# One conditional weight cast less in the slot loop of an attention and two-layer expert kernel

## The chip, the cores and the metric

The kernel runs on one core of a Trainium2 chip. The metric is the device time of one execution in microseconds (us). Engines are named as in the profile: PE (TensorE; PEld are its weight loads), DVE (VectorE), ACT (ScalarE), POOL (GpSimd), SP (SyncE, which here only issues transfers). A q behind a name is that engine's instruction queue: its branches and semaphore instructions.

## What is computed

A gated linear attention over 4 x 8 heads of 768 steps gives 3072 tokens of 384 values. A dense layer with three first matrices follows, and then a layer of eight experts, of which every token uses one:

```python
h = np.maximum(np.maximum(x @ w1, x @ w2), x @ w3)       # dense layer
x = h @ w_out
e_idx = np.argmax(x @ w_gate, axis=1)                      # expert of a token
for e in range(E):
    mask = e_idx == e
    h = np.maximum(x[mask] @ w1[e], 0.0)                   # 384 -> 1024
    out[mask] = gate_w[mask, None] * eom[mask, e, None] * (h @ w2[e])   # 1024 -> 384
```

## The kernel before

The attention and the dense layer take the first 480 us or so and are not touched. Then the tokens are sorted by expert into up to 31 slots of 128 rows; a slot holds tokens of one expert only. The slots are worked off in the order of the program text (a manual schedule: each engine executes its instructions in the order in which the code traces them).

For accuracy a float32 product is made of three products of split parts: every weight w becomes a high part (a cast on ACT, L605) and a low part (a subtraction on DVE, L606). `split1` does that for the 3 x 1024 first-layer weights of an expert in six pieces, from the landing tile s1a or s1b into w1H and w1L; `split2` does it for the second layer in eight pieces, from s2a or s2b into w2H and w2L. There is one pair w1H, w1L and one pair w2H, w2L. They are rewritten only at a slot with a new expert, under an `If`.

The last slot of an expert may hold fewer than 64 tokens. Such a slot is of kind 1 and runs alone: it multiplies the unsplit float32 weights in the landing tiles directly, in two halves of the PE array, and needs no cast. `by_kind` chooses between the two forms with an `If` on PE, ACT and DVE.

The stages of a slot j are:

- `gather` (POOL): fetch its rows; `stage` (SP): fetch its expert's weights, when they are new
- `tx`: three transposes on PE (L788), then high and low part of the rows on ACT (L793) and DVE (L794)
- `up(j, 0)` and `up(j, 1)`: first layer, columns 0 to 511 and 512 to 1023, nine matmuls each (L825), and a copy out of PSUM by ACT (L826). For a slot that runs alone the first does nothing and the second does the whole layer (L814, copy L834)
- `th`: eight transposes on PE (L865; alone L870), then `cut`: Relu on ACT (L844) and the low part on DVE (L845)
- `down`: second layer, 24 matmuls (L884; alone L814), the scaling on ACT (L898) and a scatter by POOL (L904)

They are interleaved over three slots. In iteration j of the loop the text has, in this order: `split2` pieces 0 and 1 of slot j, if new (L1152); `up(j+1, 0)`; `th(j)`; `split2` pieces 2 to 7 (L1162); the early call `cast1(j+2, 2)` (L1165); `up(j+1, 1)`; `tx(j+2)`; the fetch of s1 for slot j+3; the late call `cast1(j+2, 1)` (L1174); `down(j)`; the fetch of s2 for slot j+2.

`cast1(j, when)` is an `If` (L1132) around `split1(j)`, taken where `new[j]` equals `when`. `new[j]` is made in `slots_e` from the routing: 0 for a slot with the old expert or one that runs alone; 2 for a slot with a new expert behind a slot that runs alone; 1 for a new expert behind any other slot. The early place is open only behind a slot that runs alone, because such a slot does not read w1H and w1L. An `If` that is not taken sends, on each of its engines' queues, the semaphore signals that its body would have sent, so that whoever waits for the body goes on.

The whole program stands twice in the text, a second time for inputs with large decays; that second part is not executed here.

Of the kernel before, what the change touches and what calls it, by code (L numbers as in the profile page):

```python
# [18 lines left out]
ALU = mybir.AluOpType  # L19
# [14 lines left out]
NS = NT + NE - 1  # L34
# [50 lines left out]
def layers(tc, pool, wk, K, general, *args):  # L85
    with ExitStack() as ctx:
        _layers(ctx, tc, pool, wk, K, general, *args)


def _layers(ctx, tc, pool_, wk, K, general, qk, al, a0, v, vT, w123, wout, gates, ew1, ew2, out):  # L90

    nc = tc.nc
# [3 lines left out]
    oh, oc, rmod, rdiv, pri, io128, ioS, ioF, ut, ones, one8, pid, tno, meta, kinds, first, e0, gidx, sidx = (  # L96
        K[n] for n in ("oh", "oc", "rmod", "rdiv", "pri", "io128", "ioS", "ioF", "ut", "ones", "one8", "pid", "tno", "meta", "kinds",
                       "first", "e0", "gidx", "sidx"))
# [391 lines left out]
    def wt(shape, name, dt=F32):  # L490
        return wk.tile(shape, dt, tag=name, name=name)
# [86 lines left out]
    xg, cx, cxF, hs, ch, chg, new, eos, kind = ({} for _ in range(9))  # L578
# [29 lines left out]
    def split1(j, pieces=range(6)):  # L608
        for n in pieces:
            split(*(t[:, n % 3, n // 3 * 512:(n // 3 + 1) * 512] for t in (C["s1"][j % 2], *C["w1"])))  # L610

    def split2(j, pieces=range(NE)):
        for f in pieces:
            split(*(t[:, f] for t in (C["s2"][j % 2], *C["w2"])))
# [122 lines left out]
    def slots_e():  # L737

        end = rtmp["end"]
        rem = wt([128, NE], "rem", I32)  # L740
        nc.vector.tensor_single_scalar(rem, rtmp["ci"], 127, op=ALU.bitwise_and)
        few = wt([128, NE], "few")
        nc.vector.tensor_single_scalar(few, rem, 64.0, op=ALU.is_lt)
        lst = wt([128, NE], "lst")
        nc.vector.scalar_tensor_tensor(lst, end, isf, nfirst, op0=ALU.subtract, op1=ALU.mult)
        nc.vector.scalar_tensor_tensor(lst, end, -1.0, lst, op0=ALU.add, op1=ALU.subtract)
        wide = [128, NS, NE]
        le = wt(wide, "le", BF16)
        nc.vector.tensor_tensor(le, lst.unsqueeze(1).to_broadcast(wide), ioS.unsqueeze(2).to_broadcast(wide), ALU.is_equal)
        nc.vector.tensor_tensor(le, le, few.unsqueeze(1).to_broadcast(wide), ALU.mult)  # L750
        kd = wt([128, NS], "ff")
        nc.vector.tensor_reduce(kd, le, op=ALU.add, axis=AX.X)
        nc.vector.tensor_copy(kinds[:, :NS], kd)


        nc.vector.tensor_tensor(kinds[:, 2 * NS:], meta[:, NS:2 * NS], kd, ALU.max)
        when = wt([128, NS + 1], "eo")
        nc.vector.memset(when[:, 0:1], 1.0)
        nc.vector.tensor_scalar_add(when[:, 1:], kd, 1.0)
        nc.vector.scalar_tensor_tensor(when[:, :NS], kd, 0.0, when[:, :NS], op0=ALU.is_equal, op1=ALU.mult)  # L760
        nc.vector.tensor_tensor(kinds[:, NS:2 * NS], when[:, :NS], meta[:, NS:2 * NS], ALU.mult)

    def load_meta(j):
        chg[j] = nc.values_load(kinds[0:1, 2 * NS + j:2 * NS + j + 1], engines=(ET.SP,), min_val=0, max_val=1)
        eos[j] = nc.values_load(meta[0:1, j:j + 1], engines=(ET.SP,), min_val=0, max_val=NE - 1)

    def load_kind(j):
        kind[j] = nc.values_load(kinds[0:1, j:j + 1], engines=(ET.PE, ET.Activation, ET.DVE),
                                 min_val=0, max_val=1)
        new[j] = nc.values_load(kinds[0:1, NS + j:NS + j + 1], engines=(ET.Activation, ET.DVE),  # L770
                                min_val=0, max_val=2)

    def stage(j, both=((0, "s1"), (1, "s2"))):
        for n, s in both:
            nc.sync.dma_start(out=C[s][j % 2], in_=(ew1, ew2)[n][ds(eos[j], 1)].rearrange("o p a b -> p (o a) b"),
                              cond=(chg[j] == 1))

    def gather(j):
        xg[j] = C["cr"].tile([128, XW], F32, tag="xg", name="xg", bufs=4)
        n = TF * 128 if j < NF else NTOK  # L780
        nc.gpsimd.indirect_dma_start(out=xg[j], out_offset=None, in_=x2d[:n, :],
                                     in_offset=bass.IndirectOffsetOnAxis(ap=gidx[:, j:j + 1], axis=0),
                                     bounds_check=n - 1, oob_is_err=False)

    def tx(j):
        ps = bank(C["psT"], "T", "psT")
        for k in range(3):
            nc.tensor.transpose(ps[:, k * 128:(k + 1) * 128], xg[j][:, k * 128:(k + 1) * 128], ident)  # L788
        cx[j] = bp.tile([128, 2, DM], F32R, tag=("xH", "xL")[j % 2], name="cx")
        cxF[j] = bp.tile([128, DM], F32, tag="hH", name="cxF", bufs=7)  # L790

        def parts(hi, lo, p):
            nc.scalar.copy(hi, p)  # L793
            nc.vector.tensor_sub(lo, p, hi.bitcast(F32))  # L794

        def alone():
            nc.scalar.copy(cxF[j], ps[:, :DM])

        by_kind(j, lambda: parts(cx[j][:, 0], cx[j][:, 1], ps[:, :DM]), alone)
# [75 lines left out]
    def down(j, fs=(0, NE)):  # L875
        if fs[0] == 0:
            C["dn"] = bank(psM, "M", "psP") if j == 1 else bank(psO, "O", "psP")
        ps = C["dn"]
        w2H, w2L = C["w2"]

        def whole():
            for f in range(*fs):
                for n, (x, w) in enumerate(((0, w2H), (0, w2L), (1, w2H))):
                    mm(ps[:, :DM], ch[j][:, x, f * 128:(f + 1) * 128], w[:, f], start=(f + n == 0),  # L884
                       stop=(f == NE - 1 and n == 2))

        def alone():
            w = C["s2"][j % 2]
            for f in range(4):
                x = hs[j][:, 512 + f * 128:512 + (f + 1) * 128]  # L890
                halves(ps, DM, (x[:, :64], x[:, 64:]), (w[:, f], w[:, f + 4]), f == 0, f == 3)

        by_kind(j, whole, alone)
        if fs[1] < NE:
            return
        y = bp.tile([128, DM], F32, tag="hm", name="yo")
        gate = xg[j][:, DM:XW]
        nc.scalar.activation(y, ps[:, :DM], AF.Copy, scale=gate)  # L898
        if j in kind:
            with tc.If(kind[j] > 0):  # L900
                t = bp.tile([128, DM], F32, tag="hL", name="ylo", bufs=7)
                nc.scalar.copy(t[:64], ps[64:, :DM])
                nc.vector.scalar_tensor_tensor(y[:64], t[:64], gate[:64], y[:64], op0=ALU.mult, op1=ALU.add)
        nc.gpsimd.indirect_dma_start(out=out[:, :], out_offset=bass.IndirectOffsetOnAxis(ap=sidx[:, j:j + 1], axis=0),  # L904
                                     in_=y, in_offset=None, bounds_check=NTOK - 1, oob_is_err=False)
# [205 lines left out]
    then(slots_d)  # L1111
    then(down, 0)
    then(slots_e)

    with tc.manual_schedule() if not general else nullcontext():
# [12 lines left out]
    def guard(j):  # L1128
        return tc.If(n_all > j) if j >= NT else nullcontext()

    def cast1(j, when):
        with tc.If(new[j] == when):  # L1132
            split1(j)

    down(1, (0, 2))
# [3 lines left out]
    up(2, 0)  # L1139
    up(2, 1)  # L1140
    load_kind(NF + 1)
    load_kind(NF + 2)
    n_all = nc.values_load(meta[0:1, 2 * NS:2 * NS + 1], min_val=0, max_val=NS)
    tx(3)
    cast1(3, 1)
    down(1, (5, NE))
    for j in range(NF, NS):
        if j + 3 < NS:
            load_meta(j + 3)
            load_kind(j + 3)  # L1150
        if j > NF:
            with tc.If(new[j] > 0):  # L1152
                split2(j, range(2))
        if j + 3 < NS:
            gather(j + 3)
        with guard(j):  # L1156
            if j + 1 < NS:
                with guard(j + 1):
                    up(j + 1, 0)
            th(j)  # L1160
        if j > NF:
            with tc.If(new[j] > 0):  # L1162
                split2(j, range(2, NE))
        if j + 2 < NS:
            cast1(j + 2, 2)  # L1165
        if j + 1 < NS:
            with guard(j + 1):
                up(j + 1, 1)
                if j + 2 < NS:
                    tx(j + 2)  # L1170
        if j + 3 < NS:
            stage(j + 3, ((0, "s1"),))
        if j + 2 < NS:
            cast1(j + 2, 1)  # L1174
        with guard(j):  # L1175
            down(j)
        if j + 2 < NS:
            stage(j + 2, ((1, "s2"),))
# [50 lines left out]
```

## Time and profile before

| | us |
|---|---|
| median of three runs | 840.0 |
| the three runs | 834.53, 840.0, 840.49 |
| the profiled execution, as timed | 835.41 |
| its span, first to last instruction | 833.7 |
| PE busy | 746.9 (90%) |
| DVE busy | 380.9 (46%) |
| ACT busy | 307.0 (37%) |
| POOL busy | 110.7 (13%) |
| mean granted TensorE clock | 0.957 |

Times in the rows are microseconds from the start of the span. Busy time counts work, not branches, signals or the issue of transfers. The idle time in square brackets stands in front of an instruction, with the event that ended it; that event is inferred. The granted clock is a share of 2.4 GHz, and its two levels are 1.2 and 2.4 GHz.

### The profile page before, as it was taken

To read this page: it belongs to the slowest core of one execution; us is meant where nothing else is said; L and a number is where in the kernel's file an instruction comes from. 1 tells how busy PE (TensorE), PEld (TensorE's weight loads), DVE (VectorE), ACT (ScalarE), POOL (GpSimd) and SP (SyncE) were. 2 spreads that over 40 slices of the span, in tenths; PEclk is the share of its full clock that TensorE was granted. 3 is DMA by queue.
4 is the path that set the end of the run, shared out by engine and by line. 5 is a ranking of instruction groups with operands and counts; after the bars stand their busy time and mean duration, and the time that the engine had idled before them with its cause. 6 is when DMAs were issued, how large, how long until landed. Compare 5 with 4: busy or idle time off the path is not lost. (4 is left out here: it accounts for less than half of the span.)

```text
span 833.7 us, 14691 instructions
## 1 busy us (share of the span) xinstructions
PE 746.9 (90%) x4782; PEld 652.7 (78%) x4782; DVE 380.9 (46%) x806; ACT 307.0 (37%) x750; POOL 110.7 (13%) x117
## 2 busy tenths in 40 slices
PE   7889999989999999999999888888879798896882
PEld 7679989878999999999999777777556577763562
DVE  7868784598676474632327621110232311102322
ACT  4364343544434343432314422222444422324342
POOL 1000000010111110100103021011211201111110
PEclk9999999998999999999999999898989989999897
DMA  9732302624104140000004010115936101377450
GB/s 256 293 87 91 131 0 77 183 67 115 54 18 121 37 120 20 17 12 20 8 28 181 23 56 30 30 39 175 335 119 249 32 20 39 114 282 306 145 212 15
DMA packets 23748, 86.63 MB, mean 104 GB/s; under 512 B 7988, under 2 KB 11852, under 8 KB 19536
## 3 DMA queue, kind: packets, MB, share of 16 engines
q1 hardware_dynamic: 18192, 73.24, 26.5%
q0 software_dynamic: 3904, 10.84, 4.1%
q10 hardware_dynamic: 1536, 1.18, 0.6%
q8 instruction: 51, 0.84, 0.4%
q14 instruction: 65, 0.53, 0.2%
HBM read 128.09 MB, written 10.63 MB: 166 GB/s over the span
## 5 line engine op out<-in xcount | busy, mean ns | idle before, releaser
L429 PE MATMUL hps<-xH,wH 128*128 128x384 f32 x432 | 151.4, 350 | 1.8 <-ACT xH L341 1.8
L429 PE MATMUL hps<-xH,wL 128*128 128x384 f32 x432 | 146.1, 338 | 0.7 <-DVE wL L398 0.7
L429 PE MATMUL hps<-xL,wH 128*128 128x384 f32 x432 | 146.2, 339 | 0.4 <-DVE xL L342 0.4
L825 PE MATMUL psM<-w1H,cx 128*128 128x512 f32 x276 | 108.0, 448 | 36.6 <-ACTq L1132 36.6
L884 PE MATMUL psP<-w2H,ch 128*128 128x384 f32 x368 | 103.2, 351 | 1.4 <-ACT ch L844 1.3
L825 PEld LDWEIGHTS psM<-w1H,cx 128*128 128x128 f32 x276 | 57.6, 209 | 56.3 <-ACTq L1132 43.2
L455 POOL TENSOR_TENSOR hL<-hm,hH 128x384 fp32r<-128x384 f32 x36 | 44.8, 1244 | 404.6 <-ACT hH L450 404.5
L429 PEld LDWEIGHTS hps<-xH,wH 128*128 128x128 f32 x432 | 82.1, 190 | 8.4 <-ACT xH L341 2.5
L845 DVE SCALAR_TENSOR_TENSOR ch<-psH,ch 128x512 fp32r<-128x512 f32 x46 | 29.7, 686 | 128.6 <-ACT ch L844 128.2
L429 PEld LDWEIGHTS hps<-xH,wL 128*128 128x128 f32 x432 | 82.2, 190 | 1.0 <-DVE wL L398 1.0
L429 PEld LDWEIGHTS hps<-xL,wH 128*128 128x128 f32 x432 | 82.2, 190 | 0.9 <-DVE xL L342 0.9
L884 PEld LDWEIGHTS psP<-w2H,ch 128*128 128x128 f32 x368 | 69.8, 195 | 2.0 <-ACT ch L844 1.5
L826 ACT COPY hs<-psM 128x512 f32<-128x512 f32 x46 | 26.9, 586 | 117.2 <-PE psM L825 115.3
L825 PE MATMUL psM<-w1L,cx 128*128 128x512 f32 x138 | 62.4, 452 | 7.9 <-DVEq L1132 7.8
L465 PE MATMUL ops<-wo,hH 128*128 128x400 f32 x258 | 68.2, 345 | 0.0
L904 POOL DMA_INDIRECT out<-yo,sidx x30 | 31.2, 1041 | 275.0 <-ACTq L900 161.5
L884 PE MATMUL psP<-w2L,ch 128*128 128x384 f32 x184 | 63.1, 343 | 0.0
L436 DVE TENSOR_TENSOR hm<-hm,hps 128x384 f32<-128x384 f32 x48 | 26.4, 551 | 67.0 <-PE hps L429 63.0
L794 DVE TENSOR_TENSOR cx<-psT,cx 128x384 fp32r<-128x384 f32 x24 | 13.3, 556 | 89.0 <-ACTq L1132 88.9
L450 ACT CAST hH<-hm 128x384 fp32r<-128x384 f32 x43 | 22.0, 512 | 80.9 <-DVE hm L439 77.2
L898 ACT ACTIVATE yo<-psP,xg 128x384 f32<-128x384 f32 x30 | 17.4, 581 | 88.5 <-PE psP L884 65.2
L465 PEld LDWEIGHTS ops<-wo,hH 128*128 128x128 f32 x258 | 46.9, 188 | 0.4
(214 smaller groups left out, 1200.9 us busy)
## 6 DMA issues: line engine op xcount, KB each, us to landing
s1a<-in_ew SPq DMA_DIRECT2D x15, 1536.0 KB
s2a<-in_ew SPq DMA_DIRECT2D x15, 1536.0 KB
s1b<-in_ew SPq DMA_DIRECT2D x14, 1536.0 KB
s2b<-in_ew SPq DMA_DIRECT2D x14, 1536.0 KB
ws<-in_w SPq DMA_DIRECT2D x6, 1152.0 KB
at<-in_al SPq DMA_DIRECT2D x16, 336.9 KB
vt<-in_v SPq DMA_DIRECT2D x8, 576.0 KB
x2d<-xs SPq DMA_DIRECT2D x24, 192.0 KB
```

The costliest lines, as they stand in the source:

```text
L429: mm(ps, slab(a, f)[:, w, k], b[i][:, k], start=(n == 0), stop=(n == 8))
L436: nc.vector.tensor_max(m, m, ps)
L450: nc.scalar.copy(hH[i, f], m)
L455: (nc.gpsimd if general or i > 1 else nc.vector).tensor_sub(hL[i, f], hps["m"], hH[i, f].bitcast(F32))
L465: mm(ps[:, :DM + NG], a[i, f][:, ts_], wo[f // 3][:, b, f % 3], start=(f + n == 0), stop=(f + n == 7))
L794: nc.vector.tensor_sub(lo, p, hi.bitcast(F32))
L825: mm(ps, cx[j][:, x, ks], w[:, k, fs], start=(k + n == 0), stop=(k + n == 4))
L826: nc.scalar.copy(hs[j][:, fs], ps)
L845: nc.vector.scalar_tensor_tensor(lo, ps, 0.0, hi.bitcast(F32), op0=ALU.max, op1=ALU.subtract)
L884: mm(ps[:, :DM], ch[j][:, x, f * 128:(f + 1) * 128], w[:, f], start=(f + n == 0), stop=(f == NE - 1 and n == 2))
L898: nc.scalar.activation(y, ps[:, :DM], AF.Copy, scale=gate)
L904: nc.gpsimd.indirect_dma_start(out=out[:, :], out_offset=bass.IndirectOffsetOnAxis(ap=sidx[:, j:j + 1], axis=0), in_=y, in_offset=None, bo ...
```

## The change

The early call goes, so `cast1` has one place, behind `tx(j+2)`, and the value 2 of `new` with it; `slots_e` makes `new` in one operation where it took four.

```diff
         nc.vector.tensor_tensor(kinds[:, 2 * NS:], meta[:, NS:2 * NS], kd, ALU.max)
-        when = wt([128, NS + 1], "eo")
-        nc.vector.memset(when[:, 0:1], 1.0)
-        nc.vector.tensor_scalar_add(when[:, 1:], kd, 1.0)
-        nc.vector.scalar_tensor_tensor(when[:, :NS], kd, 0.0, when[:, :NS], op0=ALU.is_equal, op1=ALU.mult)
-        nc.vector.tensor_tensor(kinds[:, NS:2 * NS], when[:, :NS], meta[:, NS:2 * NS], ALU.mult)
+        nc.vector.scalar_tensor_tensor(kinds[:, NS:2 * NS], kd, 0.0, meta[:, NS:2 * NS], op0=ALU.is_equal, op1=ALU.mult)
...
-                                min_val=0, max_val=2)
+                                min_val=0, max_val=1)
...
-    def cast1(j, when):
-        with tc.If(new[j] == when):
+    def cast1(j):
+        with tc.If(new[j] == 1):
             split1(j)
...
-    cast1(3, 1)
+    cast1(3)
...
             with tc.If(new[j] > 0):
                 split2(j, range(2, NE))
-        if j + 2 < NS:
-            cast1(j + 2, 2)
         if j + 1 < NS:
             with guard(j + 1):
                 up(j + 1, 1)
...
         if j + 2 < NS:
-            cast1(j + 2, 1)
+            cast1(j + 2)
         with guard(j):
             down(j)
```

## Rows read from the trace of the kernel before

**Rows 1.** The page, busy time of one engine: us, share, instructions.

```profile
PE 746.9 (90%) x4782; PEld 652.7 (78%) x4782; DVE 380.9 (46%) x806; ACT 307.0 (37%) x750; POOL 110.7 (13%) x117
```

**Rows 2.** Busy time by stretch; last columns: granted clock, transfer share, GB/s.

```profile
490.00:820.00 330.00, 277.73 (x1341) 213.86 (x1340) 72.80 (x126) 109.90 (x215) 55.81 (x54) 0.93 0.38 136
508.44:521.74 13.30, 11.72 (x53) 9.94 (x53) 1.51 (x4) 3.22 (x6) 2.04 (x2) 0.87 0.08 27
548.64:560.02 11.38, 10.09 (x54) 8.69 (x54) 1.58 (x4) 3.12 (x6) 2.05 (x2) 1.00 0.09 31
```

**Rows 3.** Waits of PE, 480 to 834: us in total, times, longest.

```profile
PE psM L825 <- ACTq L1132: 36.6, 23, 3.6
PE psM L825 <- DVEq L1132: 7.8, 18, 0.7
```

**Rows 4.** Instructions of line L1132: count, ns min/median/max, first and last start.

```profile
L1132 ACTq COMPARE_BRANCH  x59: 34/45/55, 491.5 to 809.4; - x59
```

**Rows 5.** Lines L1132 and L1162 in 545 to 549; line L804, whole span.

```profile
L1132 ACTq EVENT_SEMAPHORE  x1: 17/17/17, 548.6 to 548.6; - x1
L1162 DVEq EVENT_SEMAPHORE  x1: 21/21/21, 548.9 to 548.9; - x1
L804 PEldq COMPARE_BRANCH  x144: 63/200/338, 486.6 to 814.0; - x144
```

**Rows 6.** Timeline of PE and ACT, one ordinary slot: start, duration, instruction, [idle before].

```profile
546.20 1.04 PE L865 MATMUL psH<-ident,hs 128*128 128x128 f32 x8
546.94 1.09 ACT L844 ACTIVATE ch<-psH 128x512 fp32r<-128x512 f32 x2
548.64 0.49 PE L825 MATMUL psM<-w1H,cx 128*128 128x512 f32 x1 [1.40 <-ACTq L1132]
549.28 0.51 PE L825 MATMUL psM<-w1L,cx 128*128 128x512 f32 x1 [0.15 <-DVEq L1132]
...
551.26 0.49 PE L788 MATMUL psT<-ident,xg 128*128 128x128 f32 x3
...
557.85 1.03 PE L865 MATMUL psH<-ident,hs 128*128 128x128 f32 x8
```

**Rows 7.** Timeline of PE and DVE: before the loop, and a w2 slot.

```profile
492.04 0.49 PE L825 MATMUL psM<-w1H,cx 128*128 128x512 f32 x1 [1.37 <-ACTq L1132]
...
616.11 2.89 DVE L606 TENSOR_TENSOR w2L<-s2a,w2H 128x384 fp32r<-128x384 f32 x6
617.91 0.50 PE L825 MATMUL psM<-w1H,cx 128*128 128x512 f32 x1 [3.34 <-ACTq L1132]
```

**Rows 8.** Timeline of PE and ACT, first cast of first-layer weights in the loop.

```profile
595.74 2.80 PE L814 MATMUL psP<-s2a,hs 128*64 128x384 f32 x16
596.23 3.22 ACT L605 CAST w1H<-s1a 128x512 fp32r<-128x512 f32 x6 [1.88 <-DMA s1a<-in_ew]
599.35 0.57 ACT L834 COPY hs<-psM 128x512 f32<-128x512 f32 x1
600.39 0.49 PE L825 MATMUL psM<-w1H,cx 128*128 128x512 f32 x1 [1.85 <-ACTq L1132]
601.16 0.50 PE L825 MATMUL psM<-w1L,cx 128*128 128x512 f32 x1 [0.27 <-DVEq L1132]
603.88 0.84 PE L870 MATMUL psH<-ident,hs 128*128 128x128 f32 x3
```

**Rows 9.** Timeline of PE, ACT and DVE, third cast of first-layer weights.

```profile
760.80 3.22 ACT L605 CAST w1H<-s1a 128x512 fp32r<-128x512 f32 x6 [4.76 <-DMA s1a<-in_ew]
761.45 3.70 DVE L606 TENSOR_TENSOR w1L<-s1a,w1H 128x512 fp32r<-128x512 f32 x6 [6.61 <-ACT w1H L605]
764.97 0.49 PE L825 MATMUL psM<-w1H,cx 128*128 128x512 f32 x1 [3.44 <-ACTq L1132]
...
769.07 0.79 PE L870 MATMUL psH<-ident,hs 128*128 128x128 f32 x4
```

**Rows 10.** Timeline of PE, second cast's slot.

```profile
636.26 0.39 PE L825 MATMUL psM<-w1H,cx 128*128 128x512 f32 x1
```

## Prediction

> **What bounds the kernel now.** I read the page's engine table first: PE is busy for 746.9 of 833.7 us, the other engines less than half of that [rows 1]. So time can come back only where PE stands still or runs slowly. The second view was the busy time by stretch over the slot loop, 490 to 820 us: PE is busy for 277.73 of 330 us there, and the granted clock averages 0.93 [rows 2]. That is 52 us of standing still; and as the clock has the two levels 1.2 and 2.4 GHz, a mean of 0.93 means that (1 - 0.93) / 0.5 = 14% of the stretch, 46 us, went at the lower one. The third view, PE's waits in the loop, names the cause: 36.6 us in 23 waits end with ACT's queue at L1132 and 7.8 us in 18 with DVE's queue at L1132 [rows 3]. No other entry of that view reaches 2 us.
>
> L1132 is the `If` inside `cast1`. Every slot passes it twice, by the early call (L1165, value 2) and the late one (L1174, value 1); the line has 59 branches on ACT [rows 4], and as many on DVE. To see which one holds PE, the reader should lay three views of one ordinary slot on each other. PE: the eight transposes of `th` run from 546.20 to 547.24, then PE idles 1.40 us, and the second half of the first layer (`up`, h = 1) starts at 548.64 [rows 6]. ACT: the two `cut`s of `th` occupy it from 546.94 to 548.03 [rows 6]. ACT's queue: it signals at 548.6 that it has skipped `cast1` [rows 5], and PE starts at that moment. The transposes of tx, behind which the late call stands, come only at 551.26 [rows 6], so this is the early call. What the reader should see: the early `If`, although not taken, stands in program order between `cut` and the second half, and it counts as the latest writer of w1H and w1L. PE therefore waits until ACT, then DVE, have worked off everything queued before that `If`, which has nothing to do with the weights that PE reads.
>
> In a slot that also casts second-layer weights the queue ahead of the `If` is longer: six pieces of w2 stand there, and PE waits 3.34 us [rows 7].
>
> **The change part by part.**
>
> *The skipped early `If`s.* They go, and `up(j+1, 1)` then depends on the late cast of the slot before, which both queues pass while PE is still in `down`. From the 44.4 us of L1132 waits I take off those that are no early call: 1.37 us at 492.04, before the loop's first early call, and the two places of a real cast, 1.85 and 3.44 us for ACT, with 0.27 for DVE behind the first and as much behind the second [rows 7 to 9]. Left are 37.2 us in twenty places (second halves of slots that do not run alone).
>
> *The restart of PE.* An undisturbed slot takes 11.38 us, of which PE is busy for 10.09 [rows 2]. Without a break it would need: 8.57 us from the second matmul of the second half to the next `th` (549.28 to 557.85), one more matmul of about 0.25 (549.28 to 551.26 holds eight), and 1.04 for the transposes [rows 6], in all 9.86. So each break costs 0.2 us more than its idle time, and up to 0.4 if the transposes' last tail overlaps the next matmul as it does elsewhere. I take 0.3: 20 x 0.3 = 6 us.
>
> *The clock.* A slot with a granted clock of 0.87 takes 13.30 us with 11.72 busy, against 11.38 with 10.09 at 1.00: 53 and 54 recorded matmuls, 1.63 us more [rows 2]. That the breaks cause the drops is inferred, not shown: the slow slot stands still for 13.30 - 11.72 = 1.58 us, the fast one for 1.29, and nothing else differs between them. The 46 us at the lower level cost 23 us of progress, of which 84% falls on busy PE: 19.4. About 2.7 of them belong to the two cast places and are counted there. 16.7 us remain. The bounds are nothing and all of it; I take all, since no break stays in an ordinary slot.
>
> *The real casts.* Four slots of the loop cast first-layer weights, in groups of six pieces at 596.23 [rows 8], 631, 760.80 [rows 9] and 798, all by the early call: each runs ahead of the second half's copy out of PSUM (L834), as at 596.23 against 599.35 [rows 8]. After the change ACT does that copy and the cast of tx (0.48 us) first, then the six pieces. The late skip, for which PE waits today at 600.39 until tx has been cast behind the weights, is then the cast itself, and PE can start with the first piece. At the first place `down` ends at 598.54 (595.74 + 2.80), the weights have landed at 596.23, and the first half needs 9 x 0.25 us: it ends at 600.8 instead of 603.88, a gain of 3.1 us [rows 8]. At the second the weights land only at 760.80; one piece on ACT (3.22 / 6 = 0.54) and one on DVE (3.70 / 6 = 0.62) later, at about 762.0, the low part is there, and the half ends near 764.1 instead of 769.07: 5.0 us [rows 9]. At the other two the `down` of a slot that does not run alone hides the cast now; it takes 557.85 - 551.75 - 9 x 0.25 = 3.9 us [rows 6]: the half starts at 636.26 without any wait [rows 10], and so at 802.66. Behind tx, the cast starts some 1.5 us later there, but the first pieces still come inside `down`; nothing gained or lost. Sum 8.1.
>
> *New costs.* Two ends each. The PE branch into `up(j+1, 1)` lies in the break today; PE's branches at L804 take 0.06 to 0.34 us, median 0.20 [rows 5], so 0 to 4 us in twenty. As no gap shows at the same jumps inside the continuous stretch of [rows 6], I take 1. `down(j)` next needs what the breaks gave time for: it would start at about 547.24 + 2.25 + 0.49 = 550.0, and DVE passes its last `If` before it (L1162) at 548.9 [rows 5]: 1.1 us to spare. In a w2 slot `down` would start at 617.91 - 3.34 + 2.25 + 0.49 = 617.3 and use up a piece of weights in 3.9 / 8 = 0.48 us; DVE delivers pieces 2 to 7 from 616.11 on, 2.89 / 6 = 0.48 us each [rows 7]. It stays ahead: hidden too, and I take nothing; the other end is half of the 37.2 us, 18.6, if `down` stands still in place of the second half. The operations of `slots_e` run once, before the loop: nothing.
>
> The page "Advanced Engine Details and Errata" of the Trainium skill, section Control Flow Timing, gives about 108 ns for a compare-and-branch; the trace has a median of 45 ns on ACT [rows 4], and the trace decides. If a branch's own time were all that is saved, the page's figure would make 20 x 0.11 = 2 us, an estimate.
>
> **Sum.** 37.2 + 6 + 16.7 + 8.1 - 1 = 67 us, off the profiled execution's 835.41 (span 833.7): 768.4, say 769. The median before, 840.0, lies 4.6 above that execution, so the measured gain can look larger.
>
> **Rivals.**
> - *The clock keeps dropping*, because seven alone slots and the DMA-fed casts still leave small breaks: 16.7 and 2.7 us do not come back, 835.4 - (67 - 19.4) = 788. For it: half-clock time need not have one cause. Against it: the clean slot, with a shorter break, has 1.00.
> - *The wait moves to `down`*: `cut` or the w2 cast becomes what PE waits for, 18.6 us of the waits stay, and the drops with them: 788 + 18.6 = 806. Against it the 1.1 us to spare.
> - *Only the branch is saved*: PE is really held by the cuts, which stay. Each place gives back ACT's branch, 45 ns [rows 4], and its signal, 17 ns [rows 5]: 20 x 0.06 = 1.2 us, 834.2, no change. Against it: the second half reads nothing that `cut` writes.
> - *Slower*: the signal that PE awaits is that of the late call. Then the waits stay, and the casts alone move behind tx. From copy to last low piece that is 0.48 + 0.56 + 3.70 = 4.7 us; uncovered at four places 835.4 + 19 = 854; it decides as soon as `down` covers less than 4.7, which 2.80 at two of them does. Against it: the 548.6 signal precedes that slot's tx at 551.26 [rows 5, 6].
>
> **How the numbers follow.** Likeliest 0.65 (769, its own range 756 to 782: restart, branch and clock terms at their ends, and up to 5 us for the level of the median); clock 0.20 (788); wait moved 0.06 (806); branch only 0.05 (834); slower 0.04 (854). The range 753 to 795 takes in the first two and leaves out no more than 2 in 10. About 1% is what a measurement of this kernel can tell from no change: faster 0.91, same 0.05, slower 0.04.
>
> **What would show it.** Right: no PE wait at L1132 before the second halves, slots of 9.7 to 10.1 us, clock near 1.00 over the loop, casts behind the tx cast on ACT, and the first half following `down` within a microsecond at all four. Wrong: an L884 wait for ACT or DVE of about 1 us per slot; a clock still near 0.93; a wait in front of the first halves at 636 and 802. The prediction falls as a whole if the second half still waits for ACT's queue under another line.

## The result

The kernel after takes 764.15 us (median of four runs, 762.69 to 764.72), the kernel before 837.88 (834.53 to 840.49) beside it. The ratio is 0.9119, with a 95% interval from 0.9078 to 0.9161. The forecast was 769, in 753 to 795. The profiled execution of after was timed at 764.18, its span is 762.5: 71.2 us less than the 833.7 of before, against 67 in the sum.

The page of after, where [rows 1] stood for before:

```profile
PE 716.5 (94%) x4782; PEld 636.5 (83%) x4782; DVE 380.7 (50%) x803; ACT 306.0 (40%) x750; POOL 110.9 (15%) x117
```

PE does as many instructions as before in 30 us less busy time. Some 10 us of that are restarts, since even at a clock of 1.00 a slot of before has 10.09 us busy [rows 2] and one of after 9.61; the rest is mostly the clock. The busy time by stretch of after, the slot loop (from 490 us to some 14 us ahead of the end, as in [rows 2]) and two ordinary slots; columns as there:

```profile
490.00:748.00 258.00, 246.41 (x1340) 196.85 (x1339) 72.86 (x126) 108.77 (x215) 55.88 (x54) 1.00 0.49 173
521.50:531.11 9.61, 9.61 (x55) 8.71 (x55) 1.85 (x3) 3.13 (x6) 2.03 (x2) 1.00 0.14 44
531.11:540.69 9.58, 9.58 (x54) 8.68 (x54) 1.84 (x3) 3.13 (x6) 2.05 (x2) 1.00 0.14 43
```

The loop shrinks by 72 us, from 330 to 258. PE stands still for 11.6 us of it instead of 52, and the granted clock is 1.00 instead of 0.93. An ordinary slot takes 9.6 us, all of it busy. The waits of PE in after, 480 us to the end, first entries (us in total, times, longest), beside [rows 3]:

```profile
PE psH L860 <- PEq L833: 1.7, 3, 0.6
PE psM L820 <- ACTq L1127: 1.4, 1, 1.4
PE psP L879 <- ACT ch L839: 1.4, 1, 1.4
PE psT L783 <- DMA xg<-x2d,gidx: 1.3, 1, 1.3
```

L820, L839, L860, L879 and L1127 are the old L825, L844, L865, L884 and L1132. Of the 44.4 us at the old L1132 one wait of 1.4 us is left, the one ahead of the loop. PE's timeline in an ordinary slot, to be laid beside [rows 6]:

```profile
523.60 1.04 PE L860 MATMUL psH<-ident,hs 128*128 128x128 f32 x8
524.39 0.47 PE L820 MATMUL psM<-w1H,cx 128*128 128x512 f32 x1
524.70 0.39 PE L820 MATMUL psM<-w1L,cx 128*128 128x512 f32 x1
...
526.56 0.49 PE L783 MATMUL psT<-ident,xg 128*128 128x128 f32 x3
526.81 0.42 PE L879 MATMUL psP<-w2H,ch 128*128 128x384 f32 x1
```

The second half starts at 524.39, before the last transpose has drained at 524.64, and `down` follows tx without a gap.

### The profile page after: what moved, and what is told of

Same layout as the page of the kernel before. It is cut to its first block, busy times and chain, and to the rows that moved or that the text cites. A ratio compares the mean times of both kernels' runs of the same rounds, so it can differ in the third digit from the quotient of the medians.

```text
span 762.5 us, 14586 instructions
## 1 busy us (share of the span) xinstructions
PE 716.5 (94%) x4782; PEld 636.5 (83%) x4782; DVE 380.7 (50%) x803; ACT 306.0 (40%) x750; POOL 110.9 (15%) x117
## 5 line engine op out<-in xcount | busy, mean ns | idle before, releaser
L879 PE MATMUL psP<-w2H,ch 128*128 128x384 f32 x368 | 100.1, 342 | 2.2 <-ACT ch L839 1.4
L820 PE MATMUL psM<-w1H,cx 128*128 128x512 f32 x276 | 96.5, 404 | 1.4 <-ACTq L1127 1.4
L879 PEld LDWEIGHTS psP<-w2H,ch 128*128 128x128 f32 x368 | 67.0, 188 | 3.2 <-ACT ch L839 1.6
L820 PEld LDWEIGHTS psM<-w1H,cx 128*128 128x128 f32 x276 | 51.9, 188 | 15.0 <-issue 1.8
L879 PE MATMUL psP<-w2L,ch 128*128 128x384 f32 x184 | 61.9, 337 | 0.0
L820 PE MATMUL psM<-w1L,cx 128*128 128x512 f32 x138 | 54.4, 394 | 0.1
L465 PE MATMUL ops<-wo,hL 128*128 128x400 f32 x129 | 44.3, 343 | 0.1
```

The source lines that it names most:

```text
L465: mm(ps[:, :DM + NG], a[i, f][:, ts_], wo[f // 3][:, b, f % 3], start=(f + n == 0), stop=(f + n == 7))
L820: mm(ps, cx[j][:, x, ks], w[:, k, fs], start=(k + n == 0), stop=(k + n == 4))
```

## The experiments

Eight kernels, in three groups; the kernels of a group share the runs of before on one chip. Each undoes or adds one thing.

**e2: the `If` without the weights.** Added to the kernel after, at the old place of the early call:

```diff
...
+    def idle_if(j):
+        with tc.If(new[j] == 2):
+            for n in range(6):
+                nc.scalar.copy(C["scr"][0][:, n:n + 1], pid)
+                nc.vector.tensor_sub(C["scr"][1][:, n:n + 1], pid, C["scr"][0][:, n:n + 1])
...
+        if j + 2 < NS:
+            idle_if(j + 2)
         if j + 1 < NS:
```

> The kernel after, plus an If at the place of the early call, never taken, around six copies on ACT and six subtractions on DVE of one column in two scratch tiles that PE does not read. Theory (it is the dependence of PE on w1H and w1L that costs, not the If): the cuts and the second half go on as in the kernel after, 764 plus 0 to 3 us, no new PE wait. Rival 'a second If as such costs the time': 800 to 835.

Measured: 762.97 us, ratio to before 0.9133 (0.9107 to 0.9159), no different from the kernel after. The two branches and their signals on ACT and DVE cost nothing that can be measured, as long as PE waits for nothing that the body writes. The rival "a second `If` as such" falls.

**e1: both calls, the early one in front of `th`.** The kernel before with

```diff
                     up(j + 1, 0)
+            if j + 2 < NS:
+                cast1(j + 2, 2)
             th(j)
...
-        if j + 2 < NS:
-            cast1(j + 2, 2)
```

> The kernel before, but with the early cast call standing between up(j+1, 0) and th(j) instead of behind th(j) and the second-layer casts. Both calls stay, and so do all their branches. Theory (PE's second half waits for whatever is queued on ACT and DVE ahead of the early If): only the copy of the first half is queued ahead now, so the L1132 waits before the second halves shrink from 37.2 us to under 10, the granted clock of the loop goes above 0.97, and the time is 768 to 790; the four real casts now delay the cut of th, which is the part above 764. Rival 'a second If as such costs the time' (branches, signals, code): about 835, waits unchanged. Rival 'the gain came from casting late at the four new experts': no gain or a loss, 825 to 845.

Measured: 792.54 us, ratio 0.9468 (0.943 to 0.9506): 43 us better than before with the same branches, 2.5 us above the stated 790; the granted clock of the loop is 0.96, where above 0.97 was expected. The waits of PE in e1 from 480 us on, first five (lines as in before):

```profile
PE psP L814 <- ACTq L1164: 6.5, 1, 6.5
PE psP L884 <- ACT ch L844: 4.4, 3, 1.6
PE psP L814 <- issue: 3.8, 1, 3.8
PE psM L825 <- ACTq L1132: 2.7, 5, 1.4
PE psH L865 <- ACTq L900: 1.4, 2, 0.8
```

The breaks of the ordinary slots are gone: 2.7 us are left at L1132, 1.36 of them ahead of the loop, and stretches of ordinary slots have a clock of 1.00 (505 to 552 us, 650 to 700). What is new stands at or near the slots with real casts. ACT's timeline at the third of them shows the worst:

```profile
717.36 3.22 ACT L605 CAST w1H<-s1a 128x512 fp32r<-128x512 f32 x6 [6.70 <-DMA s1a<-in_ew]
720.61 0.60 ACT L871 ACTIVATE hs<-psH 128x512 f32<-128x512 f32 x1
```

ACT stands for 6.70 us until the weights have landed and then casts, and the Relu that the slot's `down` needs is queued behind it. PE waits 6.46 us. So position decides: the same `If` costs 43 us more behind the cuts than ahead of them, although the real casts now stand in PE's way; and the same cast is free behind tx (e6), but costly ahead of work that PE is about to ask for.

**e3: the early call in front of the second-layer `If`.** The kernel before with

```diff
             th(j)
+        if j + 2 < NS:
+            cast1(j + 2, 2)
         if j > NF:
             with tc.If(new[j] > 0):
                 split2(j, range(2, NE))
-        if j + 2 < NS:
-            cast1(j + 2, 2)
```

> The kernel before, but with the early call ahead of the second-layer If (L1162) instead of behind it, still behind th. Theory: one branch and signal less ahead of it at 17 ordinary places (the L1162 signal stands 0.5 us ahead of the L1132 signal on ACT, 548.1 and 548.6) and six casts less at the three slots with second-layer casts (3.34 to 1.1 us): 835 - 17 x 0.5 - 3 x 2.3 = 819, down to 810 if some clock drops go with the shorter breaks. Rival 'a second If as such': 835. Rival 'the cuts alone are what PE waits for, whatever the If': 835 too, and the break at 548 stays at 1.4 us.

Measured: 812.48 us, ratio 0.972 (0.9681 to 0.9759). PE's two L1132 entries and two ordinary slots by stretch, in e3:

```profile
PE psM L825 <- ACTq L1132: 25.5, 23, 3.3
PE psM L825 <- DVEq L1132: 6.1, 17, 0.4
```

```profile
507.46:518.85 11.39, 10.15 (x53) 8.74 (x53) 1.84 (x4) 3.12 (x6) 2.05 (x2) 1.00 0.12 37
518.85:530.35 11.50, 10.09 (x54) 8.69 (x54) 1.85 (x4) 3.12 (x6) 2.04 (x2) 1.00 0.12 36
```

The waits fall from 44.4 to 31.6 us, 12.8 less where 8.5 + 6.9 = 15.4 were expected, and 3.6 us of them come back in front of `down`, which now waits for the second-layer casts. The time falls by more than that, 23 us, as the ordinary slots now keep a clock of 1.00, where seven of before's eleven had 0.87 (one of them is in [rows 2]). This points at the break's length as what the clock answers to, and e4 and e5 test that without any `If`.

**e4 and e5: a break without an `If`.** The kernel after, and between `th` and the second half one matmul of PE whose result nobody reads. It takes the last block of the cut's low part (e4), so that PE must wait for DVE, or of its high part (e5: index 0 instead of 1 in the first added line), so that PE waits for ACT only:

```diff
                 cut(ch[j][:, 0, h * 512:h * 512 + 512], ch[j][:, 1, h * 512:h * 512 + 512], ps)
+            x = ch[j][:, 1, 7 * 128:]
+            mm(bank(C["psR"], "R", "psw")[:, :128], x, x, start=True, stop=True)
```

> The kernel after, plus one matmul of 128 columns on PE between th and the second half that reads the last block of the low part of the cut; its result is not used. So PE stands still at the old place until DVE is through with the cut, without any If. Theory (a break there costs its length, about 0.4 us of restart and the clock): 20 breaks of 1.6 to 1.8 us and 0.1 us for the matmul, 764 + 20 x 2.1 = 806, and with the clock of the loop falling to 0.93 to 0.96 again 815 to 825. Rival 'the clock drops had another cause': granted clock of the loop above 0.98 and 800 to 808.

> The kernel after, plus the same idle matmul between th and the second half, but reading the last block of the high part of the cut. PE stands still until ACT, not DVE, is through. Theory: ACT ends some 0.85 us ahead of DVE, so the breaks are 0.8 to 1.0 us instead of 1.7; e3, whose breaks were 0.90 + 0.35 us, kept a clock of 0.97, so the drops go almost all and each break costs its length, 0.4 us of restart and 0.1 us for the matmul: 764 + 20 x 1.4 = 792, clock of the loop 0.98 or more. Rival 'any break drops the clock': clock 0.93 and 805 to 812.

Measured: e4 835.42 us, ratio to before 1.0007 (0.9973 to 1.0041); e5 802.0 us, ratio 0.9637 (0.96 to 0.9674). The waits of PE at the added matmul, and the loop and two ordinary slots by stretch, in e4:

```profile
PE psw L863 <- DVEq L1159: 31.7, 16, 3.0
PE psw L863 <- DVE ch L840: 9.6, 5, 2.7
```

```profile
490.00:819.40 329.40, 279.09 (x1357) 217.73 (x1358) 72.99 (x126) 109.55 (x215) 55.64 (x54) 0.92 0.39 136
509.26:522.66 13.40, 11.71 (x54) 10.23 (x54) 1.85 (x3) 3.22 (x6) 2.04 (x2) 0.87 0.10 30
522.66:536.15 13.49, 11.76 (x54) 10.19 (x54) 1.85 (x3) 3.22 (x6) 2.03 (x2) 0.87 0.10 32
```

and the same in e5:

```profile
PE psw L863 <- ACTq L1159: 18.4, 16, 2.2
PE psw L863 <- ACT ch L839: 5.5, 5, 1.8
```

```profile
490.00:783.10 293.10, 260.94 (x1359) 204.47 (x1358) 72.95 (x126) 108.84 (x215) 55.82 (x54) 0.98 0.44 153
507.08:518.08 11.00, 10.15 (x54) 8.92 (x55) 1.85 (x4) 3.12 (x6) 2.04 (x2) 1.00 0.12 37
518.08:529.15 11.07, 10.16 (x55) 8.88 (x55) 1.85 (x4) 3.13 (x6) 2.04 (x2) 1.00 0.12 37
```

e4 gives the whole gain back, with one `If` fewer than before: slots of 13.4 us at a clock of 0.87, the loop at 0.92, against 0.93 in [rows 2]. The price of a break can be read off e5's ordinary slots, whose clock stays at 1.00: 11.00 us against 9.61 in after, 0.85 of it the wait, leaves 0.54 for restart and idle matmul. Its span, 797.1, is 34.6 us over that of after; 23.9 of these are the 21 waits, and the other 10.7 again make 0.5 for each, though in the span they also hold what the loop's clock of 0.98 takes and other small waits that went. With 0.5 e4 should have a span of 762.5 + 41.3 + 21 x 0.5 = 814.3. It has 833.4; some 19 us are left for the clock. My expectation for e4 was 10 us short: I counted 20 breaks of 1.6 to 1.8 us, but the added matmul sits in all 21 `th` of slots that do not run alone, and in those with second-layer casts it waits up to 3.0 us. The same, with waits up to 2.2 us, puts e5's profiled execution (798.84) 7 us above the expected 792; its median is 3 us higher still. The rivals, that the drops had another cause or that any break brings them, fall: same place, same number of breaks, and at 1.7 us nine of twelve ordinary slots have a clock of 0.87, at 0.85 us none. The length alone does not decide it: three ordinary slots of e4 keep 1.00 (536.15 to 547.97, 650.59 to 662.43 and 662.43 to 674.19 us), behind breaks as long as the others.

**e6: no casts of first-layer weights.** The kernel after with

```diff
...
-        with tc.If(new[j] == 1):
+        with tc.If(new[j] == 2):
             split1(j)
```

> The kernel after with the condition of the one cast call never true: first-layer weights of the first expert stay in use for all unsplit slots, so the four casts are left out, their Ifs stay. Theory (behind tx the casts are hidden by down): 761 to 764.5, as no PE wait of the kernel after stands in front of the four first halves. Rival 'the late casts are still exposed': 754 to 759.

Measured: 761.89 us (761.25 to 765.76), ratio 0.9161 (0.9123 to 0.92), against 0.9119 for after: no difference that can be measured. The late casts are hidden; the most that better placed casts could still bring is within the noise.

**e7 and e8: the one wait that is left.** PE waits 1.37 us at 492.31 in after for the call ahead of the loop, `cast1(3)`. e7 puts that call in front of `tx(3)`:

```diff
-    tx(3)
     cast1(3)
+    tx(3)
```

> The kernel after, with the one call that stands ahead of the loop, cast1(3), traced before tx(3) instead of behind it. It is never taken here. Theory: the only wait of PE for a skipped If that is left, 1.37 us at 492.31, comes from ACT passing this If only after the cast of tx(3); it falls below 0.4 us, and the time by 1 to 1.8 us to about 762.7. Rival 'ACT passes the If late because of its register loads': the wait stays and the time is 764.

Measured: 763.29 us (760.88 to 766.05), ratio 0.9174 (0.9145 to 0.9203): nothing. The wait did not go, it changed its name. ACT and PE in e7, timeline:

```profile
486.88 0.59 ACT L821 COPY hs<-psM 128x512 f32<-128x512 f32 x1 [1.46 <-PE psM L820]
489.77 0.48 ACT L788 CAST cx<-psT 128x384 fp32r<-128x384 f32 x1 [2.30 <-ACTq L1127]
490.30 0.50 PE L820 MATMUL psM<-w1H,cx 128*128 128x512 f32 x1 [1.56 <-ACT cx L788]
```

My theory was wrong here: PE needs the cast of tx(3) itself, and ACT comes to it 2.30 us after its last work. In between its queue loads registers; one of the two lines that do it (`load_kind`), in e7 from 480 to 495 us:

```profile
L763 ACTq TENSOR_LOAD <-kinds x3: 273/287/477, 486.9 to 489.9; - x3
```

e8 traces the loads for slot 4 and for the number of slots later:

```diff
-    load_kind(NF + 2)
-    n_all = nc.values_load(meta[0:1, 2 * NS:2 * NS + 1], min_val=0, max_val=NS)
     tx(3)
     cast1(3)
+    load_kind(NF + 2)
+    n_all = nc.values_load(meta[0:1, 2 * NS:2 * NS + 1], min_val=0, max_val=NS)
```

> The kernel after, with the register loads for slot 4 and the number of slots (load_kind(4), n_all) traced behind cast1(3) instead of ahead of tx(3). In e7 the wait of PE at the first up(3, 0) stayed at 1.6 us and ended with the cast of tx(3) itself, 2.3 us after ACT was last busy; ACT's queue shows register loads of 0.28 to 0.48 us each in between. Theory now (the loads hold ACT): the wait of 1.37 us falls below 0.5 us; the time by about 1 us, which three rounds need not resolve: 762 to 764. Rival 'something else holds ACT': the wait stays at 1.4 us.

Measured: 761.61 us (760.99 to 763.28), ratio 0.9129 (0.9063 to 0.9195). The wait at the first `up(3, 0)` is no longer in the trace, and in ACT's timeline the cast follows its last copy after 0.78 us:

```profile
487.46 0.59 ACT L821 COPY hs<-psM 128x512 f32<-128x512 f32 x1 [1.45 <-PE psM L820]
488.82 0.48 ACT L788 CAST cx<-psT 128x384 fp32r<-128x384 f32 x1 [0.78 <-issue]
```

So the register loads held ACT. Whether the kernel is a microsecond faster for it the runs can't tell from 764.15, and no version tried is measurably faster than the kernel after.

## Why the prediction was right, point by point

**Which `If` holds PE.** Shown. The reading of one slot [rows 4 to 6] said the early call, by the order of signal and tx. e2 and e1 confirm it from both sides: the `If` without the dependence is free, and the dependence without the queue ahead of it is nearly so. The rivals "only the branch is saved" (834) and "the late call's signal" (854) are out with that.

**The waits, 37.2 us.** They are gone entirely, and next to nothing took their place: the 1.1 us to spare in front of `down` were real in the ordinary slots, and PE's wait for the cut (L879 for ACT, 1.4 us) is a single one, in the last slot, as before. The step "hidden too" for the slots with second-layer casts was not quite right: in two of the three PE waits a little at tx and `down`, 0.23 + 0.24 and 0.69 + 0.48 us, 1.6 in all, where nothing was charged.

**The restart, 6 us.** This term was mis-sized, at 0.3 us a break. The undisturbed slot of [rows 2] stands still for 1.29 of 11.38 us and becomes 9.61 us: 11.38 - 1.29 - 9.61 = 0.48 us a break, 9.6 us in twenty. The sum already held 10.09 - 9.86 = 0.23 for the start of the first matmul. The other 0.25 is the overlap that it put at its upper end only: without a break the second half starts 0.25 us before the last transpose has drained (524.39 against 524.64). That is also why the slots came out at 9.6 us, below the 9.7 to 10.1 that the prediction gave as a sign.

**The clock, 16.7 us.** The step "drops follow the breaks" came out: the loop of after is at 1.00, and e4 brings the drops back. But the two rows behind it do not carry it, and that taking all of the term was right is in part luck. That the fast slot stood still for less is no difference that holds: of before's eleven ordinary slots four have a clock of 1.00, and three of these stand still for as long as the slow ones or longer, 1.55 us (705.51 to 717.19), 1.71 (717.19 to 728.99) and 1.82 in this one:

```profile
496.54:508.44 11.90, 10.08 (x54) 8.68 (x54) 2.42 (x5) 3.13 (x6) 2.05 (x2) 1.00 0.11 35
```

No row is given for the 2.7 us that the prediction moves to the two cast places; their stretches, 595.74 to 603.88 at a clock of 0.90 and 758.73 to 769.07 at 0.85, make (1 - 0.90) x 8.14 + (1 - 0.85) x 10.34 = 2.4. What is left of the 71.2 us when waits, restart and casts (below) are taken off, 71.2 - 37.2 - 9.6 - 8.6 = 15.8 us, agrees with the 16.7, though it is a remainder and also holds what went the other way, the 1.6 us above and 0.84 by which a gather is waited for longer (1.28 us at 700.77, 0.44 before).

**The real casts, 8.1 us.** Timeline of PE and ACT at the first cast in after, beside [rows 8], and at the third, beside [rows 9] and the start of `down` there in before:

```profile
573.37 2.80 PE L809 MATMUL psP<-s2a,hs 128*64 128x384 f32 x16
574.10 3.22 ACT L605 CAST w1H<-s1a 128x512 fp32r<-128x512 f32 x6
576.10 0.50 PE L820 MATMUL psM<-w1H,cx 128*128 128x512 f32 x1
578.29 0.60 PE L865 MATMUL psH<-ident,hs 128*128 128x128 f32 x4
```

```profile
701.76 2.80 PE L809 MATMUL psP<-s2a,hs 128*64 128x384 f32 x16 [0.47 <-PE psT L783]
703.04 3.23 ACT L605 CAST w1H<-s1a 128x512 fp32r<-128x512 f32 x6 [1.23 <-DMA s1a<-in_ew]
704.49 0.50 PE L820 MATMUL psM<-w1H,cx 128*128 128x512 f32 x1
706.69 0.60 PE L865 MATMUL psH<-ident,hs 128*128 128x128 f32 x4
```

```profile
758.73 2.80 PE L814 MATMUL psP<-s2a,hs 128*64 128x384 f32 x16 [0.47 <-PE psT L788]
```

From the start of `down` to the end of the first half the first place takes 4.92 us, where it took 603.88 - 595.74 = 8.14: 3.2 gained, 3.1 predicted. At the third, where `down` started at 758.73 before, 4.93 instead of 10.34: 5.4 gained, 5.0 predicted. PE starts 2.0 and 1.45 us after the cast has begun, while it still runs, and at both places as `down` ends (576.17 and 704.56). So at the third it is `down` that the first half comes behind, not the low part of the first piece, as the prediction had it: the cast starts 1.28 us after `down` here, and started 2.07 us after it before. The other two places start without a wait, at 603.61 and 732.94, as they did [rows 10]. e6 says the same of all four together.

**New costs, 1 us.** Nothing: the second half starts 0.79 us after the first of the eight transposes, in step with them, so the branch into it is hidden. With 9.6 and 8.6 for 6 and 8.1, and nothing for 1, the sum comes out 5.1 us higher; the remainder of 15.8 for the clock takes 0.9 off again. That this makes the distance from 67 to 71.2 is no test, as the clock's part is what was left over.

**The rule of the Trainium skill.** The figure of the page "Advanced Engine Details and Errata" of the Trainium skill, section Control Flow Timing, for a compare-and-branch (about 108 ns) stands against 34 to 55 ns on ACT and 43 to 69 on DVE in these traces, and 63 to 338 on PE's queue for weight loads [rows 5]. e2 shows that on ACT and DVE neither matters here.

**What stays open.** Why a break of 0.90 + 0.35 us (e3) or 0.85 us (e5) leaves the clock of every ordinary slot at 1.00 and one of 1.14 + 0.42 or 1.7 us leaves it there in four of eleven (before) and three of twelve (e4): the runs show the two sides, not the rule.

## What to carry to other kernels

A conditional block that is skipped is still a writer for whoever reads its tiles: the reader waits until every engine of the block has worked off all that it has queued ahead of it. Put such a block where those queues are empty of unrelated work when the reader comes, behind the last reader and ahead of a long stretch of other work, and look for a wait that ends with a queue (ACTq, DVEq) rather than with a piece of work. Short, regular breaks of PE have to be counted with their restart and with the clock that they may take along: here 37 us of waiting cost 63, by the sum above.

## What the runs showed of the hardware

A break of PE cost about 0.5 us more than its idle time in these slots, even at the full clock (11.38 - 1.29 - 9.61 = 0.48): the drain of the matmul ahead and the start of the one behind no longer overlap others. With one break of 1.5 to 1.9 us in an ordinary slot, and PE busy for the rest, the granted clock fell to 0.87, the lower level for part of the slot, in seven of eleven ordinary slots of before and nine of twelve of e4; breaks of 0.85 us (e5) and 1.25 us (e3) brought it in none. A drop is worth about as much again as the break itself (1.63 us more, [rows 2]). And a register load from on-chip memory holds an engine's queue for 0.27 to 0.48 us: a handful of them on ACT kept PE waiting for 1.4 us.
